# First pair's output product of layer one in seven products, pair sums and attention placed first in their queues, and no elementwise work on GpSimd

## The chip, the cores and the metric

The kernel runs on one core of a Trainium2 chip. The metric is the device time of one execution in microseconds (us). In the rows PE is TensorE, PEld its weight loads, DVE is VectorE, ACT is ScalarE, POOL is GpSimd and SP is SyncE, whose queue issues nearly all transfers.

## The reference

A linear attention feeds two feed-forward layers, all in float32, on 4608 tokens of 512 numbers.

```
q_s = softmax of q over the head's 64 numbers;  k_s = softmax of k over the sequence
kv  = k_s^T v                      (8 batches, 8 heads, 576 positions)
x   = q_s kv                       -> 4608 x 512
g   = x @ w_gate;  val = x @ w_val            (512 x 1536)
x   = (g * sigmoid(g) * val) @ w_out          (1536 x 512)      layer one
h   = max(x @ w1, x @ w2, x @ w3)             (512 x 768)
out = h @ w_out2                              (768 x 512)       layer two
```

## The kernel before

The tokens are cut into nine blocks of 512. Blocks 0, 1 and 2 are worked one at a time (stages 0 to 2). The last six are worked as three pairs (3,4), (5,6), (7,8): stages 3, 4 and 5, in the code `s`. Every operand is split into a high and a low part of a 32-bit format that TensorE takes, and each product is three matmuls (high x high, high x low, low x high).

**Seven products.** A pair multiplies in Strassen's way: a block of 2 x 2 sub-matrices in seven products in place of eight, at the price of sums on DVE and ACT. `wino_unit` does that for the products with the gate, value and W1 to W3 weights: one unit is seven products of six matmuls, 42 in all, with the operands b11, t1, t3, t2, b21, b22, t4 (made by `x_wino` from the rows `xr`), and `wino_add` (L818) and `consume` (L783, L780, L774) empty the PSUM banks and put the sums together. The output product of layer one (kind "O", weight w_out) is done in one of two ways. `outs` does eight products' worth: 12 tiles x 2 halves x 4 slices x 3 matmuls = 288 matmuls. `factors` and `out_wino` do seven: 6 pairs x 7 products x 6 matmuls = 252 matmuls, with more sums around them (`eager`, `second_job`, `fourth_job`, L757, hidden parts by L799, wide operand splits by L1726 and L1729). Which stage takes which is the tuple `OUT_WINO`.

**A pair stage has four parts.** The gate part: twelve units (gate and value) with the first output products between them. The output part: the rest of the output products. The max part: nine units (W1, W2, W3) with the first products of layer two ("P") between them. The tail: the last 96 matmuls of layer two, during which DVE, ACT and POOL make the next stage's seven operands (`x_wino`: sums L1881, high parts L452, low parts L455). Beside that, "chains" work off the attention of the next blocks in slots between the products (pkv and px on PE). Stage 3 alone also makes the transformed weights, which it stores for stages 4 and 5 (`make_job`, L681 and L685).

**What sets the order.** A planner in Python places every instruction on a time line for each engine, with fixed costs (for a 128 x 512 tile: DVE 0.69, POOL 1.55, ACT 0.62), and the instructions are then written out in order of the planned times, which is the order of each engine's queue. `do` places an instruction in the first free gap, `best` on the engine that ends first (DVE or POOL, the latter only in the pair stages), and `soon` books a gap but writes the instruction at the time at which its inputs are there, ahead of what was placed before.

Of the kernel before, what the change touches and what calls it, by code (L numbers as in the profile page):

```python
# [21 lines left out]
def linear_attention_moe_moe_kernel(  # L22
# [23 lines left out]
    nc = tc.nc  # L46
# [798 lines left out]
    EASY = ()  # L845
# [186 lines left out]
    def advance(ch):  # L1032
        off = 0.45 * (ch is chains[1]) / 1.8
        while ch["steps"] and ch["steps"][0][0] != "P" and (ch["t"] <= clock[0] + LOOK[len(marks) - 1] or ch.get("bank")):
# [23 lines left out]
            elif e == "G":  # L1058
                t, i = gap("G", ch["t"] - SWITCH, dur + 2 * SWITCH)
                busy["G"].insert(i, (t, t + dur + 2 * SWITCH))  # L1060
                t = max(t + SWITCH, ch["t"])
                at(t, fn)
                ch["t"] = t + dur + LAT
            elif e == "B":
                ch["t"] = best(ch["t"], {"D": dur, "G": 2.0 * dur}, fn)
            elif e in ("D+", "D="):
                t, ch["i"] = take(ch["t"])
                ch["t"] = do("D", t, dur, fn, ch["i"])
            else:
                ch["t"] = do(e[0], ch["t"], dur, fn)  # L1070
# [271 lines left out]
    def factor_hidden_job(use, key, home):  # L1342
# [3 lines left out]
        t = max(t, use - 9.0)  # L1346
# [8 lines left out]
        t = do("A", t, 0.62, factor_hi, key, a, home)  # L1355
        there["hid", key] = t = do("D", t, 0.69, factor_lo, key, a)
# [38 lines left out]
    def second_job(use, s, p):  # L1395
        if ("B", p, 0, 1) not in have or not (p < 2 or left("or")):
            return False
# [4 lines left out]
        if p < 2:  # L1402
            a2, then = lambda: xr_slot(6 + p), None
        else:
# [17 lines left out]
    def spare_slot(p):  # L1422
        more[p] = sb.tile([128, TB], F32, tag="or", name="t2f", bufs=4)
# [6 lines left out]

    more = {}

    def spare_slot(p):
        more[p] = sb.tile([128, TB], F32, tag="or", name="t2f", bufs=4)
# [47 lines left out]
    def hidden_job(use, key):  # L1482
        if key not in ready or not left("hh"):
            return False
        t, h = acquire("hh", max(ready[key], use - 9.0))
        if use - t < HASTE and key[1:] not in EASY:
            t = soon("A", t, 0.62, hidden_hi, key)
            there["hid", key] = t = soon("D", t, 0.69, hidden_lo, key, nc.vector)
        else:
            t = do("A", t, 0.62, hidden_hi, key)  # L1490
            there["hid", key] = t = best(t, COST, hidden_lo, key, by=use - 1.5)
# [11 lines left out]
    def consumed(t, s, kind, p, i, half, a, psum):  # L1503
# [15 lines left out]
        else:  # L1519
            t = do("D", t, 0.69, consume, kind, p, i, half, a, tmp, nc.vector)  # L1520
# [8 lines left out]
    def wino_unit(s, kind, p, late_y=False, order=range(7)):  # L1529
# [3 lines left out]
        def end(op, bank, k):  # L1533
# [7 lines left out]
            elif k == 2:  # L1541
                T[1] = bank_free[bank] = do("D", max(t, T[1]), 0.69, wino_add, kind, ("t", T["i", 1]), T["i", 1], bank, nc.vector)
            elif k == 3:
                T[0] = bank_free[bank] = do("D", max(t, T[0]), 0.69, wino_add, kind, ("t", T["i", 0]), T["i", 0], bank, nc.vector)
                o = ("s", 1, 1) if kind == "W1" else ("t", T["i", 1])
                u = best(max(T[0], T[1]), COST, wino_add, kind, o, T["i", 0], T["i", 1])
# [7 lines left out]
            else:  # L1554
                C, i = ((0, 1), None) if k == 5 else ((1, 0), T["i", 0])
                t = max(t, T[0])
                if kind != "W1" and k == 5:
# [178 lines left out]
    def out_wino(s):  # L1736
# [80 lines left out]
        HOMES = ("or", "or"), ("or", "or"), ("s00", "s01"), ("s10", "s11")  # L1817
# [9 lines left out]
        for p in range(n + 1):  # L1827
            run(p, 4, after_m4)
            if p in (1, 2):
# [13 lines left out]
        for p in range(n + 1):  # L1843
            if p == 1:
                mark(split_b22)
            if 0 < p < n:
# [104 lines left out]
    def x_wino(n):  # L1951
        op, d = XOPS[n]
        t0 = max(clock[0] - 6.0, have["x"])
        for c in range(2):
            if d is None:
                dh, half = int(op[1]) - 1, int(op[2]) - 1
                split(op, c, t0, lambda dh=dh, half=half, c=c: plain_rows(dh, half, c))
# [7 lines left out]
            differ(op, c, t, lambda c=c: plain_rows(*d[0], c), b)  # L1965
# [9 lines left out]
    OUT_WINO = (4, 5)  # L1975
# [143 lines left out]
    def plan(s):  # L2119
# [7 lines left out]
        if wide:  # L2127
            mark(lambda: at(clock[0], new_rows))
        for p in range(F1 // 2):
            if p == 2:  # L2130
                mark(lambda: begin_x(s + 1))
            for n, kind in enumerate("GV"):
                wino_unit(s, kind, p)
                if p and wide:
                    if p < F1 // 2 - 1:
                        factors(s, p - 1, 2 * n, (("acc0", "acc1"), ("acc2", "acc3"))[n])
                    if n and p < F1 // 2 - 1:
# [203 lines left out]
```

## Time and profile before

| | us |
|---|---|
| median of 3 runs (1518.18 to 1522.36) | 1520.64 |
| the profiled execution | 1522.33 |
| its span, first to last instruction | 1520.5 |
| PE busy in the span | 1458.5 (96%) |
| DVE busy | 1097.2 (72%) |
| ACT busy | 697.2 (46%) |
| POOL busy | 80.4 (5%) |

The profiled execution lies 1.7 us above the median, and 1.8 us of it lie outside the span. PE's busy time counts a matmul to its modelled end, so it hides short waits; the time of a stage is better read as the number of its matmuls times their distance, plus what is lost.

### The profile page before, as it was taken

The page shows a single profiled execution, that of the slowest core. Times are in us where ns is not written, and L with a number is a line of the kernel's source. Part 1 is how long each engine was busy: PE and PEld are TensorE (multiplying, and loading weights), DVE is VectorE, ACT ScalarE, POOL GpSimd, SP SyncE. Part 2 cuts the span into 40 slices and gives each one's busy share as a digit, 9 for nine tenths or more (in the row PEclk, how much of TensorE's full clock was granted, in tenths as well). Part 3 has the DMA queues.
Part 4 walks back from the last instruction along what each step waited for, and adds up shares of the span by engine and source line. Part 5 has one row for each costly group of instructions (what it writes and reads, how often), then busy time and mean ns, then how long its engine had stood idle before and what let it go on. Part 6 is the DMA issues. An engine that isn't in the chain of part 4 may idle for free.

```text
span 1520.5 us, 20625 instructions
## 1 busy us (share of the span) xinstructions
PE 1458.5 (96%) x6834; PEld 1177.2 (77%) x6834; DVE 1097.2 (72%) x1879; ACT 697.2 (46%) x1196; POOL 80.4 (5%) x70
## 2 busy tenths in 40 slices
PE   2899999999999999999999989999999999999998
PEld 1666688888878888878877867888877778888887
DVE  7869996787777678676579885677887755578553
ACT  3758774554566535535443344334532332245112
POOL 1000000000000000000012040000000300000000
PEclk9899999999999999999999999999999999999999
DMA  7798878878788899988578777775776576657764
GB/s 193 201 274 298 275 235 231 257 238 256 217 283 269 289 372 307 280 268 238 180 215 259 222 221 202 209 207 160 222 207 173 177 223 195 191 160 220 208 202 148
DMA packets 318729, 349.01 MB, mean 230 GB/s; under 512 B 158368, under 2 KB 197280, under 8 KB 318624
## 3 DMA queue, kind: packets, MB, share of 16 engines
q1 hardware_dynamic: 313824, 346.52, 75.2%
q10 hardware_dynamic: 4800, 1.18, 0.4%
q8 instruction: 55, 0.90, 0.3%
q14 instruction: 50, 0.41, 0.1%
HBM read 257.16 MB, written 90.44 MB: 229 GB/s over the span
## 4 chain that ended last, share of the span: by engine, by line
PE 78%; DVE 8%; DMA 6%; ACT 5%; issue 2%; SPq 1%; ACTq 0%; DVEq 0%
PE pb L715 52%; PE pacc L736 11%; PE pacc L748 4%; PE pb L736 4%; PE pb L748 3%; DMA stage<-in_moe_w_out_dram 1%; PE pkv L270 1%; PE pacc L728 1%; ACT plain L528 1%; DMA plain<-raw_V 1%; DVE hlo L803 1%; DVE tall L818 1%; DMA v_sb<-in_v_dram 1%; DMA stage<-in_moe_w_gate_dram 1%; ACT L774 1%
## 5 line engine op out<-in xcount | busy, mean ns | idle before, releaser
L715 PE MATMUL pb<-b11h,wall 128*128 128x512 f32 x756 | 270.1, 398 | 13.1 <-ACT wall L565 6.4
L818 DVE TENSOR_TENSOR tall<-tall,pb 128x512 f32<-128x512 f32 x234 | 159.9, 684 | 158.6 <-PE pb L715 146.7
L715 PE MATMUL pb<-b21h,wall 128*128 128x512 f32 x756 | 265.1, 393 | 0.0
L715 PEld LDWEIGHTS pb<-b11h,wall 128*128 128x128 f32 x756 | 142.7, 189 | 50.6 <-ACT wall L565 8.4
L715 PEld LDWEIGHTS pb<-b21h,wall 128*128 128x128 f32 x756 | 143.1, 189 | 30.7 <-ACT tall L808 0.4
L808 ACT COPY tall<-pb 128x512 f32<-128x512 f32 x117 | 68.8, 588 | 196.8 <-PE pb L715 158.6
L715 PE MATMUL pb<-b11l,wall 128*128 128x512 f32 x378 | 148.6, 393 | 0.0
L715 PE MATMUL pb<-b21l,wall 128*128 128x512 f32 x378 | 148.0, 391 | 0.0
L568 DVE TENSOR_TENSOR wall<-plain,wall 128x512 fp32r<-128x512 f32 x126 | 86.5, 689 | 38.1 <-ACT wall L565 37.5
L565 ACT CAST wall<-plain 128x512 fp32r<-128x512 f32 x126 | 77.1, 618 | 63.8 <-DVE plain L547 22.8
L736 PE MATMUL pacc<-hhi,ow 128*128 128x512 f32 x304 | 98.9, 389 | 0.1
L715 PE MATMUL pb<-t3h,wall 128*128 128x512 f32 x252 | 88.5, 392 | 3.0 <-DVE tall L818 2.9
L789 ACT CAST hhi<-tall 128x512 fp32r<-128x512 f32 x74 | 45.5, 618 | 98.3 <-DVE tall L783 79.1
L736 PE MATMUL pacc<-ow,hhi 128*128 128x512 f32 x288 | 89.0, 390 | 0.0
L715 PE MATMUL pb<-t1h,wall 128*128 128x512 f32 x252 | 88.8, 393 | 0.0
L715 PE MATMUL pb<-b22h,wall 128*128 128x512 f32 x252 | 88.7, 392 | 0.0
L715 PE MATMUL pb<-t2h,wall 128*128 128x512 f32 x252 | 88.5, 392 | 0.0
L715 PE MATMUL pb<-t4h,wall 128*128 128x512 f32 x252 | 88.0, 390 | 0.0
L715 PEld LDWEIGHTS pb<-b11l,wall 128*128 128x128 f32 x378 | 71.4, 189 | 15.2 <-issue 1.2
L715 PEld LDWEIGHTS pb<-b21l,wall 128*128 128x128 f32 x378 | 71.5, 189 | 14.5
L783 DVE TENSOR_TENSOR tall<-s,pb 128x512 f32<-128x512 f32 x81 | 54.9, 679 | 19.4 <-PE pb L715 15.1
L803 DVE TENSOR_TENSOR hlo<-tall,hhi 128x512 fp32r<-128x512 f32 x69 | 49.5, 718 | 26.4 <-ACT hhi L789 25.8
(279 smaller groups left out, 3001.5 us busy)
## 6 DMA issues: line engine op xcount, KB each, us to landing
wall<-wino_W SPq DMA_DIRECT2D x153, 256.0 KB, 3.1
wall<-wino_G SPq DMA_DIRECT2D x102, 256.0 KB, 3.2
wall<-wino_V SPq DMA_DIRECT2D x102, 256.0 KB, 3.0
ow<-parts_O SPq DMA_DIRECT2D x33, 512.0 KB, 5.5
ow<-parts_P SPq DMA_DIRECT2D x32, 512.0 KB, 5.1
wino_W<-wall SPq DMA_DIRECT2D x63, 256.0 KB, 4.5
ow<-owino SPq DMA_DIRECT2D x48, 256.0 KB, 3.5
wino_G<-wall SPq DMA_DIRECT2D x42, 256.0 KB, 4.4
```

What stands on the lines that cost most here:

```text
L270: nc.tensor.matmul(out=c["pkv"][u * D:(u + 1) * D, g, :], lhsT=lhsT, rhs=rhs, start=i == 0, stop=i == R,)
L528: nc.scalar.activation(out=plain[conv[i]], in_=high.bitcast(F32), func=AF.Abs, scale=2.0 ** -112)
L565: nc.scalar.copy(out=wall[:, i:i + 2, 0], in_=plain[kind, f].rearrange("p (a n) -> p a n", a=2))
L568: eng.tensor_tensor(out=wall[:, i:i + 2, 1], in0=plain[kind, f].rearrange("p (a n) -> p a n", a=2), in1=wall[:, i:i + 2, 0], op=ALU.subtract,)
L715: nc.tensor.matmul(out=banks[bank], lhsT=a, rhs=b, start=start and n == 0, stop=stop and n == 5, skip_group_check=True,)
L736: nc.tensor.matmul(out=banks[bank], lhsT=lhsT, rhs=rhs, start=first and n == 0, stop=last and n == 2)
L748: nc.tensor.matmul(out=banks[bank[e]], lhsT=w[:, a, es], rhs=h[b], start=first and n == 0, stop=last and n == 2, skip_group_check=True,)
L783: eng.tensor_tensor(out=hidden_tile(kind, f, half, tmp), in0=s, in1=a(), op=ALU.mult if kind == "V" else ALU.max)
L789: nc.scalar.copy(out=hid[key][0], in_=st["h", key[1], key[2], key[3]])
L803: eng.tensor_tensor(out=lo, in0=st.pop(("h", key[1], key[2], key[3])), in1=hi, op=ALU.subtract)
L808: nc.scalar.copy(out=tall[:, i], in_=banks[bank])
L818: eng.tensor_tensor(out=out_, in0=tall[:, x], in1=banks[bank] if isinstance(bank, str) else tall[:, bank], op=ALU.add)
```

## The change

It has four pieces. `OUT_WINO` becomes (3, 4, 5): the first pair does its output product in seven products too, with places of its own for two kinds of temporary tiles (in stage 3 the tiles t2f stand in s00 to s11, because the slots "or" are taken by the weights). `best` never takes POOL. `wino_add` and, from stage 3 on, `consume` are placed by `soon`; so are the steps of the attention chains in stages 3 and 4 (`HURRY`). The rest keeps the order of the shared buffers right ("hid order", "x end").

```diff
-    EASY = ()
+    HURRY = (3, 4)
...
-        if alone[0]:
-            engines = engines.replace("G", "")
+        engines = engines.replace("G", "")
         e = min(engines, key=lambda e: gap(e, t, cost[e])[0] + cost[e] + (0.4 if e == "G" else 0.0))
         return do(e, t, cost[e], fn, *a, ENG[e])
...
             elif e in ("D+", "D="):
                 t, ch["i"] = take(ch["t"])
-                ch["t"] = do("D", t, dur, fn, ch["i"])
+                ch["t"] = (soon if len(marks) - 1 in HURRY else do)("D", t, dur, fn, ch["i"])
             else:
-                ch["t"] = do(e[0], ch["t"], dur, fn)
+                ch["t"] = (soon if len(marks) - 1 in HURRY else do)(e[0], ch["t"], dur, fn)
...
+        elif tight:
+            t = max(t, have["s read"])
+            at(t - 0.01, spare_slot, p, ("s00", "s01", "s10", "s11")[p - 2])
+            a2, then = lambda: more[p], None
...
-            t = do("D", t, 0.69, consume, kind, p, i, half, a, tmp, nc.vector)
+            t = (soon if s > 2 else do)("D", t, 0.69, consume, kind, p, i, half, a, tmp, nc.vector)
+        have["s read"] = max(have.get("s read", 0.0), t)
...
-                T[1] = bank_free[bank] = do("D", max(t, T[1]), 0.69, wino_add, kind, ("t", T["i", 1]), T["i", 1], bank, nc.vector)
+                T[1] = bank_free[bank] = soon("D", max(t, T[1]), 0.69, wino_add, kind, ("t", T["i", 1]), T["i", 1], bank, nc.vector)
...
-                u = bank_free[bank] = do("D", t, 0.69, wino_add, kind, o, T["i", 0], bank, nc.vector)
+                u = bank_free[bank] = soon("D", t, 0.69, wino_add, kind, o, T["i", 0], bank, nc.vector)
...
-        HOMES = ("or", "or"), ("or", "or"), ("s00", "s01"), ("s10", "s11")
+        HOMES = (("or", "or") if s > 3 else None,) * 2 + (("s00", "s01"), ("s10", "s11"))
...
-            if p in (1, 2):
+            if s == 3 and p < 4:
+                ahead("second", 2.0, second_job, s, (5, 4, 2, 3)[p])
+            elif s > 3 and p in (1, 2):
                 ahead("second", 2.0, second_job, s, n - 2 + p)
...
-    OUT_WINO = (4, 5)
+    OUT_WINO = (3, 4, 5)
```

The tail of stage 3 on DVE, before (h_7685 and h_7996 are hidden tiles of layer two, k_sb and km belong to the attention, the operands b11 to t4 are those of stage 4):

```order
L455 TENSOR_TENSOR b11l<-xr,b11h 128x512
L803 TENSOR_TENSOR hlo<-tall,hhi 128x512
L455 TENSOR_TENSOR t1l<-tall,t1h 128x512
L1881 TENSOR_TENSOR tall<-xr 128x512
L455 TENSOR_TENSOR t1l<-tall,t1h 128x512
L803 TENSOR_TENSOR hlo<-h_7685,hhi 128x512
L455 TENSOR_TENSOR t3l<-tall,t3h 128x512 x2
```

The same place after the change (L1891 is the line that was L1881):

```order
L455 TENSOR_TENSOR b11l<-xr,b11h 128x512 x2
L803 TENSOR_TENSOR hlo<-tall,hhi 128x512
L1891 TENSOR_TENSOR tall<-xr 128x512 x2
L455 TENSOR_TENSOR t1l<-tall,t1h 128x512 x2
L803 TENSOR_TENSOR hlo<-h_7770,hhi 128x512
L1891 TENSOR_TENSOR tall<-xr 128x512 x2
L455 TENSOR_TENSOR t3l<-tall,t3h 128x512
L161 TENSOR_TENSOR tall<-k_sb 128x512
L162 TENSOR_TENSOR km<-tall 128x256
L455 TENSOR_TENSOR t3l<-tall,t3h 128x512
```

The sums L1881 that POOL did now stand in DVE's queue, between the low parts.

The start of stage 4 on ACT, before: L774 is the gate's Silu, L218 the attention's Exp, and pb_8239 is the bank that the second unit's first product waits for.

```order
L774 ACT_TABLE_LOAD
L774 ACTIVATE s<-tall 128x512
L218 ACT_TABLE_LOAD
L218 ACTIVATE k_sb<-k_sb 128x512
L774 ACT_TABLE_LOAD
L774 ACTIVATE s<-pb_8239 128x512
```

After the change (the bank is pb_8299):

```order
L218 ACTIVATE k_sb<-k_sb 128x512
L774 ACT_TABLE_LOAD
L774 ACTIVATE s<-tall 128x512
L218 ACT_TABLE_LOAD
L218 ACTIVATE k_sb<-k_sb 128x512
L218 ACTIVATE kr_sb<-kr_sb 64x256
L774 ACT_TABLE_LOAD
L774 ACTIVATE s<-pb_8299 128x512
```

One Exp moved ahead of the first Silu, and one more small Exp (kr_sb) now stands between the two Silus.

The start of stage 3's output part on DVE after the change, which before held the plain output product's few instructions (t2f and the tiles h and xr are parts of the seven products' operands, k_sb and kr_sb the attention's):

```order
L799 TENSOR_TENSOR hlo<-h_5536,hhi 128x512
L204 TENSOR_TENSOR k_sb<-k_sb,kb 128x1024
L799 TENSOR_TENSOR hlo<-h_5756,hhi 128x512
L757 TENSOR_TENSOR xr<-tall 128x512
L799 TENSOR_TENSOR hlo<-h_5982,hhi 128x512
L757 TENSOR_TENSOR t2f<-h_6613,xr 128x512
L209 TENSOR_TENSOR kr_sb<-kr_sb,kb 64x256
L799 TENSOR_TENSOR hlo<-h_6225,hhi 128x512
L757 TENSOR_TENSOR t2f<-h_6411,xr 128x512
```

Each low part (L799) is what one output product waits for, and a sum or a step of the attention stands between one and the next.

Counted over the whole program, PE has 36 matmuls of 128 x 512 fewer; POOL loses all its 35 elementwise instructions; DVE gains 71 instructions; SP gains 16 transfers, since 42 loads of 256 KB take the place of 26 (22 of 512 KB and 4 of 256 KB).

## Rows read from the trace of the kernel before

**Rows 1.** Windows, stages 1, 3, 4 and 5: length, busy time and instructions, clock, DMA.
```profile
core 0: us, PE busy (x) PEld busy (x) DVE busy (x) ACT busy (x) POOL busy (x), PEclk, DMA share, GB/s
155.00:310.00 155.00, 154.79 (x769) 124.22 (x768) 126.33 (x227) 99.81 (x172) 2.13 (x2) 1.00 0.81 242
584.26:912.84 328.58, 318.05 (x1524) 257.59 (x1522) 243.52 (x424) 145.88 (x282) 45.01 (x29) 0.99 0.78 240
912.84:1226.27 313.43, 304.67 (x1396) 248.14 (x1395) 228.89 (x356) 125.10 (x202) 19.61 (x12) 0.99 0.69 197
1226.27:1520.50 294.23, 290.46 (x1279) 239.52 (x1277) 170.16 (x250) 88.95 (x146) 0.00 (x0) 1.00 0.65 190
```

**Rows 2.** Chain that ended last: start us, us, what, stages 4 and 5.
```profile
933.18 1.32 PE pkv L270 x40
...
1397.79 38.08 PE pb L715 x168
```

**Rows 3.** Timeline of PE, one px step: start us, us, instruction.
```profile
786.39 0.28 PE L433 MATMUL px<-qthi,kvhi 128*128 128x256 f32 x1
...
787.19 0.39 PE L715 MATMUL pb<-t4h,wall 128*128 128x512 f32 x1
```

**Rows 4.** Windows, the four parts of stage 3, then of stage 4.
```profile
584.26:732.36 148.10, 146.71 (x746) 120.49 (x744) 103.27 (x195) 71.36 (x134) 9.85 (x8) 1.00 0.83 257
732.36:773.77 41.41, 40.68 (x210) 32.40 (x209) 19.83 (x35) 20.57 (x38) 1.69 (x2) 1.00 0.73 226
773.77:885.73 111.96, 107.56 (x476) 87.12 (x475) 96.04 (x168) 42.12 (x89) 18.10 (x12) 0.98 0.72 217
885.73:912.84 27.11, 23.10 (x98) 17.58 (x96) 24.38 (x27) 11.83 (x22) 15.37 (x10) 1.00 0.84 258
912.84:1045.20 132.36, 130.42 (x634) 106.93 (x632) 84.99 (x143) 51.98 (x81) 1.06 (x1) 0.99 0.73 198
1045.20:1091.54 46.34, 46.34 (x206) 38.22 (x204) 38.27 (x56) 26.87 (x43) 0.00 (x0) 1.00 0.68 213
1091.54:1199.47 107.93, 104.54 (x463) 85.44 (x462) 83.43 (x136) 33.33 (x55) 5.40 (x3) 1.00 0.64 180
1199.47:1226.27 26.80, 23.37 (x98) 17.55 (x97) 22.21 (x24) 12.92 (x25) 13.15 (x8) 1.00 0.71 237
```

**Rows 5.** Waits of PE in stages 3 and 4: us in total, times, longest.
```profile
PE pb L736 <- DVE hlo L803: 5.0, 5, 1.6
PE pb L715 <- DVE tall L818: 2.9, 3, 1.2
PE pb L715 <- DVE t2l L455: 2.3, 1, 2.3
...
PE pb L715 <- ACT s L774: 1.9, 1, 1.9
```

**Rows 6.** Window with POOL busy throughout, in the tail of stage 3.
```profile
885.10:900.00 14.90, 13.27 (x59) 10.56 (x58) 14.83 (x12) 5.40 (x10) 14.86 (x9) 1.00 0.71 215
```

**Rows 7.** Timeline of DVE inside that window.
```profile
886.90 0.68 DVE L818 TENSOR_TENSOR tall<-tall,pb 128x512 f32<-128x512 f32 x1
...
890.31 1.77 DVE L803 TENSOR_TENSOR hlo<-tall,hhi 128x512 fp32r<-128x512 f32 x1
```

**Rows 8.** Groups of DVE in stage 4's output part: busy us, mean ns, idle before.
```profile
L799 DVE TENSOR_TENSOR hlo<-h,hhi 128x512 fp32r<-128x512 f32 x14 | 9.7, 690 | 4.2 <-ACT hhi L796 4.0
...
L1729 DVE TENSOR_TENSOR b11l<-tall,b11h 128x1024 fp32r<-128x1024 f32 x1 | 1.2, 1228 | 0.3 <-ACT b11h L1726 0.3
```

**Rows 9.** Timeline of ACT at the start of stage 4.
```profile
919.93 0.63 ACT L774 ACTIVATE s<-tall 128x512 f32<-128x512 f32 x1 [2.23 <-DVE tall L818]
920.58 1.28 ACT L218 ACT_TABLE_LOAD   x1
921.87 0.63 ACT L218 ACTIVATE k_sb<-k_sb 128x512 f32<-128x512 f32 x1
922.52 1.28 ACT L774 ACT_TABLE_LOAD   x1
923.81 0.60 ACT L774 ACTIVATE s<-pb 128x512 f32<-128x512 f32 x1
```

**Rows 10.** Windows, just after PE's waits for Silu and for t2l.
```profile
925.50:928.90 3.40, 3.40 (x10) 2.63 (x9) 0.69 (x1) 2.19 (x3) 0.00 (x0) 0.50 0.28 81
782.30:785.60 3.30, 3.30 (x8) 2.62 (x9) 3.30 (x7) 0.00 (x0) 0.00 (x0) 0.50 0.40 136
```

More of the change, by code (lines that the diff above doesn't have):

```diff
@@ L1345, in factor_hidden_job @@
         t, a, then = ready[key]
-        t = max(t, use - 9.0)
+        t = max(t, use - 9.0, 0.0 if home else have.get("hid order", 0.0))
         if home == ("or", "or"):
@@ L1355, in factor_hidden_job @@
         t = do("A", t, 0.62, factor_hi, key, a, home)
+        if not home:
+            have["hid order"] = t - 0.62 - LAT + 0.01
         there["hid", key] = t = do("D", t, 0.69, factor_lo, key, a)
@@ L1395, in second_job @@
     def second_job(use, s, p):
-        if ("B", p, 0, 1) not in have or not (p < 2 or left("or")):
+        tight = s == 3
+        if ("B", p, 0, 1) not in have or not (p < 2 or tight or left("or")):
             return False
@@ L1420, in linear_attention_moe_moe_kernel, with spare_slot @@
     more = {}
-    def spare_slot(p):
-        more[p] = sb.tile([128, TB], F32, tag="or", name="t2f", bufs=4)
+    def spare_slot(p, tag="or"):
+        more[p] = sb.tile([128, TB], F32, tag=tag, name="t2f", bufs=4 if tag == "or" else 1)
     def fourth_job(use, p):
@@ L1484, in hidden_job @@
             return False
-        t, h = acquire("hh", max(ready[key], use - 9.0))
-        if use - t < HASTE and key[1:] not in EASY:
+        t, h = acquire("hh", max(ready[key], use - 9.0, have.get("hid order", 0.0)))
+        if use - t < HASTE:
+            have["hid order"] = t + 0.01
             t = soon("A", t, 0.62, hidden_hi, key)
@@ L1490, in hidden_job @@
             t = do("A", t, 0.62, hidden_hi, key)
+            have["hid order"] = t - 0.62 - LAT + 0.01
             there["hid", key] = t = best(t, COST, hidden_lo, key, by=use - 1.5)
@@ L1541, in end @@
             elif k == 2:
[L1542 removed]
+                T[1] = bank_free[bank] = soon("D", max(t, T[1]), 0.69, wino_add, kind, ("t", T["i", 1]), T["i", 1], bank, nc.vector)
             elif k == 3:
[L1544 removed]
+                T[0] = bank_free[bank] = soon("D", max(t, T[0]), 0.69, wino_add, kind, ("t", T["i", 0]), T["i", 0], bank, nc.vector)
                 o = ("s", 1, 1) if kind == "W1" else ("t", T["i", 1])
[L1546 removed]
+                u = T["c22"] = best(max(T[0], T[1]), COST, wino_add, kind, o, T["i", 0], T["i", 1])
                 if kind == "W1":
@@ L1556, in end @@
                 t = max(t, T[0])
+                if k == 6:
+                    t = max(t, T["c22"], T["c12"])
                 if kind != "W1" and k == 5:
@@ L1845, in out_wino @@
                 mark(split_b22)
-            if 0 < p < n:
+            if 0 < p < n and HOMES[p - 1]:
                 ahead("hid2", 2.0, factor_hidden_job, (s, "O", p + 1, 6), HOMES[p - 1])
@@ L1956, in x_wino @@
                 dh, half = int(op[1]) - 1, int(op[2]) - 1
-                split(op, c, t0, lambda dh=dh, half=half, c=c: plain_rows(dh, half, c))
+                have["x end"] = max(
+                    have.get("x end", 0.0), split(op, c, t0, lambda dh=dh, half=half, c=c: plain_rows(dh, half, c))
+                )
                 continue
@@ L1964, in x_wino @@
                 b = lambda c=c: plain_rows(*d[1], c)
-            differ(op, c, t, lambda c=c: plain_rows(*d[0], c), b)
+            have["x end"] = max(have.get("x end", 0.0), *differ(op, c, t, lambda c=c: plain_rows(*d[0], c), b))
     def x_plain(j, dh):
@@ L2127, in plan @@
         if wide:
-            mark(lambda: at(clock[0], new_rows))
+            mark(lambda: at(max(clock[0], have["x end"]), new_rows))
         for p in range(F1 // 2):
```

7 lines of the change are left out of this document (3 added, 4 removed).

## The prediction

> **What bounds the kernel now.** I read the busy shares first: PE 96%, DVE 72%. PE bounds the kernel, so the time is its matmuls plus what PE loses. Stages 0 to 2 keep their PE order, and the additions to DVE, ACT and SP begin with stage 3, so I look at stages 3 and 4 [rows 1]. Stage 5 has no POOL work and takes 294.2 us with its 1278 matmuls (289.7) and the last stores, so it loses almost nothing; I leave it as it is [rows 1].
>
> What a stage loses comes from counting. In an undisturbed run 168 matmuls take 38.08 us, 0.2267 us each [rows 2]. A pkv step of the attention costs 1.32 us [rows 2], a px step 0.80 (786.39 to 787.19) [rows 3], or 0.68 where it is one piece of three matmuls. Stage 3 has 21 units of 42, 288 output and 144 layer-two matmuls: 1314, or 297.8 us; four pkv and eight px steps add 11.7. Its length is 328.6 us [rows 1], so **19.0 us are lost**. Stage 4 has 36 matmuls fewer (289.7 us), two pkv and eight px steps (8.5), and 313.4 us: **15.2 us lost**. By parts, in the same way [rows 4]: stage 3's gate part 2.7 (624 matmuls, three pkv), output part 2.0 (168, one pkv), max part 9.0 (426, eight px), tail 5.35 (96); stage 4's 4.6 (552, two pkv), 0.1 (204), 5.5 (426, eight px) and 5.0 (96).
>
> Which waits these are is in the list of PE's waits [rows 5]: 5.0 us for low parts of hidden tiles (L803, all in the tails), 2.9 for PSUM sums (L818), 2.3 once for t2l, 1.9 once for Silu. Then the clock: right after the t2l wait and right after the Silu wait the granted clock is 0.50, that is 1.2 GHz, for 3.3 and 3.4 us [rows 10]. Half of that, some 1.7 us each, is lost behind either wait.
>
> Why DVE is late in the tails: while POOL works without pause from 885.1 to 900, DVE is busy 14.83 of 14.90 us with only 12 instructions [rows 6]. A subtraction of two SBUF tiles takes 1.77 us there; a sum that takes one operand from PSUM takes its usual 0.68 [rows 7]. Undisturbed, the former takes 0.69 [rows 8]. So 12 instructions worth 8.3 us cost 14.8: POOL's 14.9 us cost DVE 6.5, and its nine tiles in that window would have cost DVE 6.2 itself. POOL's help there is worth nothing.
>
> **The change part by part.**
>
> *Seven products in stage 3.* 288 matmuls become 252: 36 x 0.2267 = **8.2 us less on PE**. Transfers: 42 loads of 256 KB take the place of 24 tiles' 512 KB, 10.8 for 12.6 MB. That stage's DMA share is 0.78 now, and the shares of stages 3 to 4 are under stage 1's 0.81, where PE was fed [rows 1]; I cost the 16 more issues on SP's queue at nothing. If that cover goes, one late load of an output weight would cost what any wait in the list does, 1 to 2 us.
>
> *What DVE takes on.* The order shows 71 instructions more, POOL's 35 among them. They are 57 of 128 x 512 at 0.69, 15 of 128 x 1024 at 1.22 [rows 8], less two short copies: 57 us. Of these 8 belong to stage 4 (POOL's 11 there), so 49 to stage 3. Against that the stretching goes. POOL's 45.0 us in stage 3 [rows 1] at the rate found (6.5 per 14.9) are at most 20 us; five all-reduces are in it, so I take 18. DVE in stage 3: 243.5 + 49 - 18 = 274.5 us. In a stage of about 309 us that is 89%.
>
> Does PE wait at 89%? The nearest rows: stage 1 has 81.5% with PE busy 154.79 of 155 us, and stage 4's output part 83% with 0.1 us lost [rows 1, 4]. On the other side is the window in which DVE was full: PE was busy 13.27 of 14.90, 11% idle [rows 6]. The heaviest place is stage 3's output part, where one low part per product (1.36 us of PE) stands beside sums, four steps of the attention and the first weights of W1. Stage 4 does its own there in 38.3 us of 46.3 [rows 4]; some 7 us come on top, so about 45 in 47.5. Bounds for this part: 0.1, and 11% of 47.5 = 5.2; I take 2.0, since the low parts run up to three tiles ahead of PE.
>
> *Sums and attention first.* `soon` moves no work. It takes the PSUM sums (2.9 us of waits) and the attention out from behind other work; what stands behind them are low parts, weights' low parts (L685) and hidden parts, which have more slack. Together with POOL gone, stage 3's max part loses its t2l wait with its half clock (4.0 of 9.0: those operands now come out of the output part as in stage 4, where nothing is lost at that seam) and most of the rest. Bounds 0.1 (the clean part of stage 4) and the present 9.0 and 5.5; I take 2.0 and 1.7.
>
> *The tails.* From b11l on DVE has in stage 3 now 28 tile instructions and 2 us of attention, 21 us at 0.69, and starts at about 888, between the two instructions of [rows 7]. It ends near 909; t4, the last operand, is needed when six products of the next stage are done, 885.7 + 21.8 + 6 x 1.36 = 915.7. The low parts of the hidden tiles stand between the sums; the last three come some 10 us in, when their products are due from about 14 us in. Bounds 0.1 and the present 5.35 and 5.0; I take 0.8 and 0.7.
>
> *The gate parts.* At the start of stage 4 the second unit's first product waits for Silu out of its bank. The row order there is Silu, table load, Exp, table load, Silu [rows 9]: that ends 11.6 us after the stage's start, when its first unit takes 9.5. After the change the second (small) Exp stands in that row as well: 0.4 more by size (bounds 0 and a full Exp's 0.63). So this wait stays, 2.4 for 2.1, and the half clock behind it too: 4.6 becomes 5.0. In stage 3's gate part DVE is fuller, but its sums go first: 2.7 becomes 3.0.
>
> On ACT's tables the Trainium skill (ScalarE: Activation LUTs, What ACT_TABLE_LOAD costs) says that a switch takes 1.28 us for the load and 1.38 more for a drain. Here the load takes 1.28 and the next instruction starts 0.01 us later [rows 9], so the drain does not show; by the page the three loads would end about 2.8 us later and the time would be 1498.
>
> *Sum.* Stage 3 keeps 3.0 + 2.0 + 2.0 + 0.8 = 7.8 of 19.0; stage 4 keeps 5.0 + 0.1 + 1.7 + 0.7 = 7.5 of 15.2. Gain: 8.2 + 11.2 + 7.7 = 27.1 us. The profiled execution took 1522.3 (1.8 of it outside its span, 1.7 above the median): 1522.3 - 27.1 = **1495 us**.
>
> **The rivals.**
>
> *DVE becomes what PE waits for in stage 3, and new waits there are as long as the old.* For it: 89% is above every long stretch in which PE was fed. Against it: the planner's 0.69 and 0.62 agree with the undisturbed rows, and what it did not know, POOL's cost to DVE, is gone. Then only 8.2 + 7.7 remain: 1506 (1502 to 1514).
>
> The Trainium skill (Perfetto Trace Analysis, Optimizing Scalar/DVE Operations) speaks for this rival: with DVE saturated, moving work to ScalarE or even GpSimd may make sense; it adds that the two share a read port, so that it might not help. The trace bears out the second half (1.77 for 0.69); with the first half the time is that rival's 1506.
>
> *DVE can't keep up at all, and the kernel is slower.* If in-order waits (DVE standing before an Exp that waits for its table, 1.28 us [rows 9], with bank sums behind it) hold DVE to a usable share u, stage 3 takes 274.5/u. It eats up stage 4's gain when it takes 336.3, that is at u = 82%, about what stages 1 and 4 show as possible at least. At u = 78% stage 3 takes 352 and the kernel 1538.
>
> *Nearly all losses go*, only the Silu wait and its clock stay: stage 3 keeps 2.8, stage 4 5.3, gain 34 us, 1488 or less.
>
> *The order changes and the waits don't:* the tails' waits come from ACT, not DVE. Of PE's tail waits 5.0 us end with DVE's L803 [rows 5], so I give it little; the kernel would still save the 8.2: 1514, the slow end of the first rival.
>
> **How the numbers follow.** Forecast (1488 to 1502) 0.60; DVE-limited stage 3 (1502 to 1514) 0.22; nearly all losses go (under 1488) 0.08; no change (within 0.3%, 4.6 us, about what a measurement of this kernel can tell from none) 0.05; slower 0.05. Faster is 0.60 + 0.22 + 0.08 = 0.90. The range 1485 to 1510 leaves out about 0.05 below and 0.13 above.
>
> **What would show it.** Right: POOL's row holds only memsets and all-reduces; no subtraction on DVE above 0.75 us; in stage 3 36 matmuls fewer, L803 gone from the tails' waits, stage 3 at 308 to 311 us and stage 4 at 305 to 307; one wait of 2.3 to 2.5 us for Silu at stage 4's start with the clock at 0.50 behind it. Wrong: waits of PE for L799 or L685 in stage 3's output and max parts, a second stretch at 0.50 behind one of them, DVE over 95% there. A gap for DMA before an output product would say that the smaller loads come late.

## The result and the profile after

The changed kernel takes 1501.42 us (median of 4 runs, 1500.72 to 1502.07) against 1520.63 of the kernel before (1518.18 to 1522.36): a ratio of 0.9875, 95% interval 0.9858 to 0.9892, so 19.2 us faster. Its profiled execution took 1501.56, of which the span is 1499.5. The forecast was 1495.0 with a range of 1485 to 1510; the time lies in the range and 6.4 us above the forecast, and 19.2 us were gained where the sum had 27.1.

The page's busy row and its row of PE's granted clock in 40 slices (9 is 90% or more), of the changed kernel:

```profile
PE 1443.3 (96%) x6798; PEld 1169.4 (78%) x6798; DVE 1110.1 (74%) x1950; ACT 702.0 (47%) x1204; POOL 23.9 (2%) x35
...
PEclk9899999999999999999999999999999999999999
```

PE has 36 matmuls fewer (6834 before), and POOL holds memsets and all-reduces alone, 35 instructions. Next, windows of the changed kernel: stages 3, 4 and 5, then the four parts (gate, output, max, tail) of stage 3 and of stage 4; the columns are those of [rows 1]. In stage 3 the gate part now has 552 matmuls where it had 624, and the output part 204 for 168, so these two are compared by what they lose and not by their length.

```profile
582.84:893.01 310.17, 305.54 (x1487) 250.23 (x1486) 260.84 (x479) 152.43 (x291) 6.06 (x4) 1.00 0.80 244
893.01:1204.26 311.25, 304.17 (x1396) 250.01 (x1394) 225.49 (x370) 123.20 (x202) 2.12 (x2) 0.99 0.69 202
1204.26:1499.50 295.24, 290.67 (x1279) 239.45 (x1277) 168.20 (x250) 88.92 (x146) 0.00 (x0) 1.00 0.63 191
...
582.84:713.96 131.12, 130.39 (x673) 106.96 (x672) 106.89 (x207) 66.79 (x128) 4.10 (x3) 1.00 0.87 262
713.96:761.97 48.01, 48.01 (x245) 39.25 (x244) 42.58 (x71) 31.62 (x55) 1.96 (x1) 1.00 0.73 213
761.97:871.21 109.24, 105.34 (x476) 86.08 (x474) 92.79 (x173) 41.75 (x85) 0.00 (x0) 1.00 0.74 231
871.21:893.01 21.80, 21.80 (x97) 17.94 (x96) 18.57 (x31) 12.27 (x23) 0.00 (x0) 1.00 0.84 267
893.01:1029.81 136.80, 131.95 (x634) 108.06 (x633) 87.07 (x147) 49.46 (x80) 2.12 (x2) 0.98 0.72 200
1029.81:1076.05 46.24, 46.24 (x206) 38.29 (x205) 38.23 (x56) 26.78 (x43) 0.00 (x0) 1.00 0.69 215
1076.05:1182.50 106.45, 104.22 (x464) 85.64 (x462) 81.24 (x139) 33.64 (x55) 0.00 (x0) 1.00 0.64 182
1182.50:1204.26 21.76, 21.76 (x98) 18.02 (x96) 18.94 (x31) 13.33 (x24) 0.00 (x0) 1.00 0.79 282
```

Stage 3 took 328.58 us [rows 1] and takes 310.17, inside the 308 to 311 of the forecast. Stage 4 took 313.43 and takes 311.25, where 305 to 307 was forecast. Both tails are clean now: 96 matmuls of 0.2267 us are 21.76, and they take 21.80 and 21.76 (27.11 and 26.80 in [rows 4]). Stage 4's gate part is the one that became longer: 132.36 in [rows 4], 136.80 now.

The waits of PE from stage 3 on, us in total, times, longest:

```profile
PE pb L715 <- ACT tall L827: 2.6, 1, 2.6
PE pb L715 <- DVE b21l L1737: 2.5, 3, 1.0
PE pb L715 <- ACT s L774: 2.2, 1, 2.2
PE pb L715 <- DVE tall L818: 2.2, 3, 1.5
PE px L433 <- DVE tall L818: 1.7, 2, 0.9
```

Against [rows 5] the 5.0 us of low parts (L803) and the 2.3 for t2l are gone. The Silu wait (L774) is there, as forecast. Two entries of over 2 us are new. One is ACT's row copy L827. The other is b21l, once in each of stages 3, 4 and 5.

The first, on ACT's timeline at the start of stage 4 (start us, us, instruction; in brackets the wait ahead of it and what ended it):

```profile
891.87 1.07 ACT L827 COPY tall<-pb 128x512 f32<-128x512 f32 x2 [1.12 <-DMA out_dram<-tall]
...
897.88 0.58 ACT L827 COPY tall<-pb 128x512 f32<-128x512 f32 x1 [3.90 <-DMA out_dram<-tall]
...
904.61 0.63 ACT L774 ACTIVATE s<-tall 128x512 f32<-128x512 f32 x1 [3.06 <-DVE tall L818]
905.26 1.28 ACT L218 ACT_TABLE_LOAD   x1
906.56 0.63 ACT L218 ACTIVATE k_sb<-k_sb 128x512 f32<-128x512 f32 x1
907.10 0.40 ACT L218 ACTIVATE kr_sb<-kr_sb 64x256 f32<-64x256 f32 x1
907.51 1.28 ACT L774 ACT_TABLE_LOAD   x1
908.80 0.60 ACT L774 ACTIVATE s<-pb 128x512 f32<-128x512 f32 x1
```

The copy that empties a bank of stage 3's last products stands 3.90 us, until a store of an earlier copy has left the slot in which it wants to write. The first product of t3 needs that bank. PE meets this wait and the Silu wait as follows (timeline of PE):

```profile
895.51 0.39 PE L715 MATMUL pb<-t1h,wall 128*128 128x512 f32 x1
898.52 0.50 PE L715 MATMUL pb<-t3h,wall 128*128 128x512 f32 x1 [2.63 <-ACT tall L827]
...
906.85 0.39 PE L715 MATMUL pb<-t4h,wall 128*128 128x512 f32 x1
909.46 0.79 PE L715 MATMUL pb<-b11h,wall 128*128 128x512 f32 x1 [2.22 <-ACT s L774]
```

Counted from where the next matmul would have started, 0.23 us after the last, PE loses 2.78 and 2.38 us.

Windows behind these two waits, and for contrast behind one of 1.46 us (L818) in stage 4's max part; the column after POOL is the granted clock:

```profile
899.10:902.40 3.30, 3.30 (x9) 2.59 (x8) 1.01 (x2) 2.40 (x3) 0.00 (x0) 0.50 0.43 130
909.60:912.90 3.30, 3.30 (x8) 2.60 (x9) 0.41 (x1) 0.84 (x2) 0.00 (x0) 0.52 0.01 4
1110.80:1114.10 3.30, 3.30 (x15) 2.73 (x16) 3.19 (x9) 0.59 (x1) 0.00 (x0) 1.00 0.97 294
```

Behind either long wait the clock is at 1.2 GHz for nearly all of the 3.3 us, and 8 or 9 matmuls stand where 15 stand at 2.4 GHz. The length of a wait does not tell this by itself: in the kernel with eight products below, PE loses 2.54 us by the same count to a load at 665, in stage 3's gate part, and from 667.5 to 670.8 its clock is 1.00.

### The profile page after: what moved, and what is told of

Its sections match the earlier page's. It is cut to its first block, busy times and chain, and to the rows that moved or that the text cites. A ratio compares the mean times of both kernels' runs of the same rounds, so it can differ in the third digit from the quotient of the medians.

```text
span 1499.5 us, 20638 instructions
## 1 busy us (share of the span) xinstructions
PE 1443.3 (96%) x6798; PEld 1169.4 (78%) x6798; DVE 1110.1 (74%) x1950; ACT 702.0 (47%) x1204; POOL 23.9 (2%) x35
## 4 chain that ended last, share of the span: by engine, by line
PE 78%; DVE 5%; ACT 3%; DMA 3%; issue 1%; SPq 1%; ACTq 0%; DVEq 0%
PE pb L715 52%; PE pacc L736 10%; PE pacc L748 6%; PE pb L748 5%; PE pb L736 3%; PE pkv L270 1%; DVE tall L818 1%; DMA plain<-raw_V 1%; ACT L218 1%; PE px L434 1%; PE px L435 1%; PE px L433 1%; ACT L774 0%; DMA twos<-sums_W 0%; DMA qown<-in_q_dram 0%
## 5 line engine op out<-in xcount | busy, mean ns | idle before, releaser
L818 DVE TENSOR_TENSOR tall<-tall,pb 128x512 f32<-128x512 f32 x234 | 159.8, 684 | 165.3 <-PE pb L715 151.1
L715 PEld LDWEIGHTS pb<-b21h,wall 128*128 128x128 f32 x756 | 141.9, 188 | 29.7
L748 PE MATMUL pacc<-hhi,ow 128*128 128x512 f32 x248 | 82.0, 389 | 0.0
L783 DVE TENSOR_TENSOR tall<-s,pb 128x512 f32<-128x512 f32 x81 | 55.0, 680 | 18.0 <-PE pb L715 14.4
L748 PE MATMUL pb<-hhi,ow 128*128 128x512 f32 x216 | 68.3, 390 | 0.0
L789 ACT CAST hhi<-tall 128x512 fp32r<-128x512 f32 x62 | 38.4, 620 | 63.4 <-DVE tall L783 48.3
```

The lines of the kernel that those rows point to most:

```text
L715: nc.tensor.matmul(out=banks[bank], lhsT=a, rhs=b, start=start and n == 0, stop=stop and n == 5, skip_group_check=True,)
L748: nc.tensor.matmul(out=banks[bank[e]], lhsT=w[:, a, es], rhs=h[b], start=first and n == 0, stop=last and n == 2, skip_group_check=True,)
L783: eng.tensor_tensor(out=hidden_tile(kind, f, half, tmp), in0=s, in1=a(), op=ALU.mult if kind == "V" else ALU.max)
L789: nc.scalar.copy(out=hid[key][0], in_=st["h", key[1], key[2], key[3]])
L818: eng.tensor_tensor(out=out_, in0=tall[:, x], in1=banks[bank] if isinstance(bank, str) else tall[:, bank], op=ALU.add)
```

## The experiments

Each set of runs had the kernel before in it, with medians of 1519.3 to 1520.6 us. So where two kernels come from different sets, as the changed kernel and those below do, up to some 1.4 us of a difference can be due to that. Times of stages are those of one profiled execution.

**GpSimd back.** Everything else as in the changed kernel; `best` may take POOL in the pair stages again.

```diff
-        engines = engines.replace("G", "")
+        if alone[0]:
+            engines = engines.replace("G", "")
```

> The changed kernel with one piece undone: in the pair stages the planner may choose GpSimd again (it then gives it 54 tile operations, more than the 35 of before, since DVE has more to do). Theory of the prediction: GpSimd's work stretches DVE's two-SBUF-input operations from 0.69 to 1.77 us, so the tails of stages 3 and 4 lose 4 to 6 us each again and the max parts some more: 1511 to 1520. Rival, DVE-limited stage 3: relief for DVE, which is at 89% there, outweighs it: 1495 to 1501.

Measured: 1531.07 us, ratio to the kernel before 1.0073 (1.0057 to 1.0088). That is 29.7 us more than the changed kernel, beyond either expectation. POOL has 63 elementwise instructions, where 54 were expected. The busy line of its page, and two of DVE's groups in stages 3 and 4:

```profile
PE 1454.8 (95%) x6798; PEld 1171.6 (77%) x6798; DVE 1127.5 (74%) x1892; ACT 696.0 (45%) x1197; POOL 129.7 (8%) x98
...
L818 DVE TENSOR_TENSOR tall<-tall,pb 128x512 f32<-128x512 f32 x156 | 106.4, 684 | 90.5 <-PE pb L715 81.2 <-ACT wall L681 5.6 <-ACT tall L808 1.9
L803 DVE TENSOR_TENSOR hlo<-tall,hhi 128x512 fp32r<-128x512 f32 x8 | 9.9, 1234 | 4.2 <-ACT hhi L789 4.2
```

DVE has 58 instructions fewer than in the changed kernel (1950) and is busy 17.4 us longer (1110.1). The low parts L803 of the tiles tall, with two SBUF operands, take 1234 ns where the changed kernel has 680 (8.2 us for 12 in the same stages); other groups with two such operands are lengthened less (L783 into h 965 for 692, L803 of the tiles h 773 for 687). The sums with one operand in PSUM take 684, as without POOL (683). What PE waits for most are DVE's instructions (L818 13.4 us in four entries, hlo of L803 3.9, qtlo 3.3), and no entry is POOL's.

**No "first".** All `soon` that the change brought are `do` again.

```diff
-            t = (soon if s > 2 else do)("D", t, 0.69, consume, kind, p, i, half, a, tmp, nc.vector)
+            t = do("D", t, 0.69, consume, kind, p, i, half, a, tmp, nc.vector)
...
-                u = bank_free[bank] = soon("D", t, 0.69, wino_add, kind, o, T["i", 0], bank, nc.vector)
+                u = bank_free[bank] = do("D", t, 0.69, wino_add, kind, o, T["i", 0], bank, nc.vector)
```

> The changed kernel with one piece undone: bank-emptying sums and attention are placed by do, as before, in place of soon. Theory of the prediction: the order is worth a few us, mostly in the max parts (waits for L818): 1503 to 1508. Rival, the order carries most of the gain: 1511 or more. Second rival, the order hurts: sums written ahead of an operand's low part make PE wait 0.8 to 1.0 us for b21l in each of the three stages, so that without it the kernel is at 1497 to 1500.

Measured: 1500.75 us, ratio 0.9881 (0.9866 to 0.9896): no different from the changed kernel, and outside all three expectations. But the stages differ: by the starts of their first products, stage 3 takes 318.2 us (310.2 with "first") and stage 4 302.6 (311.3). The profiled execution took 1504.9, 4.2 above the median; ahead of stage 3 it was 5.8 us longer than the changed kernel's. No wait for b21l is left, as the second rival said, but in stage 3 longer ones for L818 and L783 stand in the max part. In this pair of kernels the order is worth 8 us in stage 3, and stage 4 is 8.6 longer with it; the next experiment shows that this 8.6 does not belong to the order as such.

**Eight products.** `OUT_WINO = (4, 5)`.

> The changed kernel with one piece undone: stage 3 does its output product in eight products' worth of matmuls again. Theory of the prediction: 36 matmuls come back, 8.2 us, and DVE is freer, which gives back little: 1508 to 1512. Rival, DVE-limited stage 3: the 29 us of sums taken off DVE give back as much as the matmuls cost: 1499 to 1503.

Measured: 1509.81 us, ratio 0.9933 (0.9917 to 0.9950). In all, the seven products are worth 8.4 us; the forecast had 8.2. By stages it is another sum. The windows of stages 3 and 4 of this kernel:

```profile
584.32:911.06 326.74, 317.38 (x1524) 257.80 (x1522) 234.64 (x442) 148.43 (x286) 4.90 (x4) 0.99 0.76 239
911.06:1213.82 302.76, 300.52 (x1395) 247.82 (x1394) 224.80 (x370) 122.73 (x201) 2.13 (x2) 1.00 0.70 205
```

With seven products stage 3 is 16.6 us shorter, twice what the 36 matmuls are, and stage 4 is 8.5 longer. Here stage 4 has the sums first too and neither the wait for L827 nor the one for Silu at its start: its gate part takes 128.2 us for 136.8.

**The kernel before without GpSimd.** The unconditional replacement of the first experiment, put into the kernel before.

> The kernel before with one piece alone: the planner never chooses GpSimd. Theory of the prediction: the tails' losses of 5.35 and 5.0 us go, and the max parts lose some 2 to 5 us less: 1506 to 1511. Rival: DVE's longer queue makes new waits of the same size: 1517 to 1522.

Measured: 1513.95 us, ratio 0.9959 (0.9944 to 0.9974), 5.3 us less than the kernel before beside it (1519.26) and between the two expectations. The tails shrink from 27.1 and 26.8 to 23.5 and 21.8 us, but the Silu wait at stage 4's start grows to 3.9 us, and stage 3's max part gains nothing (113.4 us). Against the kernel with eight products above, which differs in the order "first" and the plumbing that goes with the change, stage 3 takes 325.6 us here for 326.7 and stage 4 308.4 for 302.8: with eight products stage 3 gains nothing by the order, and it is stage 4 that is shorter with it.

**The slot of the row copies.** Who makes the new wait? The planner gives a slot back 2.5 us after the copy, when the store is to be issued; here it counts on 5 us more.

```diff
-            drop(i, sync(t + 2.5, store_rows, j, m, i))
+            drop(i, sync(t + 2.5, store_rows, j, m, i) + 5.0)
```

> Kernel after, with one number changed: the planner counts the slot of a stored row copy as free 5 us later, so the next copy into the same slot is planned later. My theory (the 2.78 us that PE loses at 895.74 in stage 4's gate part come from a row copy, L827 on ACT, that stands 3.90 us before a store still reading its slot, with the next casts behind it): this wait and the half clock behind it go, 2.8 + 1.7 = 4.5 us less, stage 4 at about 306.8 us and the kernel at 1497. Rival (that cast is late since DVE's or ACT's row is full there, and the store only ends last): another wait of 2 to 3 us takes its place before the same products, stage 4 stays at 310 to 312 and the kernel at 1500 to 1503.

Measured: 1498.03 us, ratio 0.9856 (0.9843 to 0.9869). Stage 4's window:

```profile
894.34:1201.13 306.79, 302.31 (x1395) 248.94 (x1394) 224.80 (x369) 122.49 (x200) 2.13 (x2) 0.99 0.69 204
```

Stage 4 is 4.5 us shorter, as expected of the wait and its half clock, and no wait took its place there. The kernel gained 3.4; the rest went in one late load in stage 3's tail and in the start (0.7 later).

**The seam to the max part.** DVE's timeline of the changed kernel ahead of b21l in stage 3:

```profile
764.81 1.23 DVE L1737 TENSOR_TENSOR t2l<-xr,t2h 128x1024 fp32r<-128x1024 f32 x1 [0.18 <-ACT t2h L1734]
765.96 0.68 DVE L1714 TENSOR_TENSOR xr<-pacc,xr 128x512 f32<-128x512 f32 x1
766.56 0.68 DVE L818 TENSOR_TENSOR tall<-tall,pb 128x512 f32<-128x512 f32 x1
767.15 1.22 DVE L757 TENSOR_TENSOR xr<-xr 128x1024 f32<-128x1024 f32 x1
768.29 0.68 DVE L818 TENSOR_TENSOR tall<-tall,pb 128x512 f32<-128x512 f32 x1
768.88 1.22 DVE L1737 TENSOR_TENSOR b21l<-xr,b21h 128x1024 fp32r<-128x1024 f32 x1
```

Two bank sums stand ahead of b21l, which PE waits for at 769.02. The first max unit alone gets plain order:

```diff
+        put = soon if tuple(order) == tuple(range(7)) else do
...
-                u = bank_free[bank] = soon("D", t, 0.69, wino_add, kind, o, T["i", 0], bank, nc.vector)
+                u = bank_free[bank] = put("D", t, 0.69, wino_add, kind, o, T["i", 0], bank, nc.vector)
```

> Kernel after, but in the first max unit of each stage the bank sums are put in plain planned order, no longer first, so that b21l stands ahead of them on DVE. My theory (the waits for b21l of 1.13, 0.93 and 0.93 us at the start of the max parts of stages 3, 4 and 5 come from sums that were put ahead of it): all three go, about 3.0 us less, the kernel at 1498.5. Rival (the sums that now come later hold up their banks, or b21l is late anyway): the waits stay or change their name to L818, the kernel at 1500 to 1503.

Measured: 1501.90 us, ratio 0.9882 (0.9864 to 0.9900): nothing. The three waits for b21l are gone, and stage 5 is 1.4 us shorter (290.1 to the end of its last product), but stage 3 takes 318.0 for 310.2. Its waits from the max part to the next stage's first units:

```profile
PE px L433 <- DVE tall L818: 4.5, 4, 2.0
PE pb L715 <- DVE tall L818: 2.2, 1, 2.2
PE pb L736 <- DVE hlo L803: 2.0, 2, 1.7
```

The sums that came later hold the next products: the rival was right in stage 3, my theory in stage 5. Stage 4 takes 305.4 us for 311.3, though its own max part is 1.3 longer: the waits for L827 and for Silu at its start are both gone, and the edit says nothing of them. They come and go with what stands before them.

**Keys later.** The last pair's keys start 24 us later, so that their Exps leave the place between the first Silus.

```diff
-        chains[2]["t"] = clock[0]
+        chains[2]["t"] = clock[0] + 24.0 * (s == 5)
```

> Kernel after, but the chain of the keys in the last pair starts 24 us later, so that no Exp with its two table loads stands between the first two Silus of stage 4. My theory (the Silu wait is those two loads of 1.28 us and the Exp): the wait of 2.38 us at 907.08 and the half clock behind it go, some 4 us less, the kernel at 1497 to 1498. Rival (the Exps, moved, make another Silu or sum late, or the attention comes late for its px steps): a wait of 2 to 4 us shows up later in stage 4, the kernel at 1500 to 1504.

Measured: 1494.17 us, ratio 0.9831 (0.9817 to 0.9844), 7.3 us less than the changed kernel, more than expected. ACT's timeline at the start of stage 4, and the stage's window:

```profile
899.44 1.28 ACT L774 ACT_TABLE_LOAD   x1
901.50 0.63 ACT L774 ACTIVATE s<-tall 128x512 f32<-128x512 f32 x1 [0.78 <-DVE tall L818]
902.04 0.58 ACT L774 ACTIVATE s<-pb 128x512 f32<-128x512 f32 x1
...
893.60:1196.45 302.85, 300.62 (x1396) 247.73 (x1394) 225.40 (x372) 120.80 (x198) 2.13 (x2) 1.00 0.71 206
```

One table load stands where three stood, and the second Silu follows the first by 0.54 us instead of 4.19. PE does not wait for L827 any more either, although nothing was done to the stores; how the slots changed hands there was not followed up. Both waits with both half clocks are 2.78 + 2.38 + 2 x 1.7 = 8.6 us, and stage 4 is 8.4 shorter, with the sums and the attention still first in it.

**The three together.**

> The three edits before this one together: slot kept 5 us longer, bank sums of the first max unit in plain order, keys of the last pair 24 us later. If the three waits have separate causes the gains add up: 4.5 + 3.0 + 4.0 = 11.5 us, the kernel at about 1490, which is what the forecast's rival of nearly all losses gone would have been. Rival (the waits share DVE's and ACT's full rows at the start of stage 4, so that taking one away lengthens another): half of that or less, 1495 to 1501.

Measured: 1496.23 us, ratio 0.9844 (0.9827 to 0.9860), 5.2 us less than the changed kernel and 2.1 more than with the late keys alone, in the rival's range. Stage 4 takes 301.7 us and stage 5 289.8 to the end of its last product, both as the theory wants, but stage 3 has 314.3: the seam's plain order costs there again, and not at the start of stage 4, where the rival looked for it.

**The three, with plain order at the seam in stages 4 and 5 alone.**

```diff
+        put = soon if s == 3 or tuple(order) == tuple(range(7)) else do
```

> Kernel after with the keys of the last pair 24 us later, the slot of row copies kept 5 us longer, and plain order for the bank sums of the first max unit in stages 4 and 5 alone (stage 3 keeps them first). My theory (each stage is decided by its own order: stage 3 wants the sums first, stages 4 and 5 don't): stage 3 at about 310, stage 4 at 302, stage 5 at 290, against 310.2, 302.9 and 291.8 with the late keys alone: 2 to 3 us less than that kernel, 1491 to 1492. Rival (what plain order gains there was made by the other order in stage 3): stages 4 and 5 as with the late keys alone, 1494 to 1495.

Measured: 1490.76 us, ratio 0.9813 (0.9800 to 0.9826). This is 10.7 us below the changed kernel and 29.0 below the kernel before beside it (1519.73), just under the 1491 to 1492 of the theory. Its windows of stages 3, 4 and 5, then of stage 4's gate part:

```profile
583.14:892.96 309.82, 305.37 (x1487) 250.50 (x1486) 261.69 (x479) 153.55 (x292) 6.07 (x4) 1.00 0.80 246
892.96:1194.62 301.66, 300.66 (x1396) 247.74 (x1394) 226.06 (x372) 121.31 (x198) 2.13 (x2) 1.00 0.71 208
1194.62:1488.10 293.48, 289.84 (x1279) 239.76 (x1277) 168.55 (x250) 88.93 (x146) 0.00 (x0) 1.00 0.64 191
...
892.96:1021.16 128.20, 128.20 (x633) 105.97 (x632) 87.62 (x149) 47.53 (x76) 2.13 (x2) 1.00 0.76 212
```

Stage 4's gate part has PE busy without a pause. Most of the gain was there with the late keys alone (1494.17); stage 4 is 1.2 and stage 5 2.0 us shorter than in that kernel. The time is close to the 1488 of the prediction's rival in which nearly all losses go.

**Seven products alone; first alone.** Why does GpSimd cost 5.3 us in the kernel before and 29.7 in the changed one? These two complete the eight combinations: the first undoes both other parts, the second is GpSimd back together with eight products.

> The kernel before with the seven products alone: GpSimd may take work in pairs, sums and attention in plain order. Theory A (GpSimd's harm grows with DVE's load: the seven products bring some 50 us of elementwise work into stage 3, and GpSimd then stretches DVE where it is full): slower than before or no gain, stage 3 some 325 us or more, the kernel at 1520 to 1530. Theory B (GpSimd's harm in the kernel with its work put back comes from putting sums first, which shifts what GpSimd has taken): the seven products give their 8 us here too, 1510 to 1514.

Measured: 1508.67 us, ratio 0.9929 (0.9917 to 0.9941).

> The kernel before with sums and attention first alone: eight products in the first pair's output, GpSimd may take work in pairs. Theory A (GpSimd's harm grows with DVE's load): about as before, 1517 to 1522, since the order by itself is worth nothing. Theory B (putting sums first makes GpSimd's harm larger): 1528 to 1538.

Measured: 1539.20 us, ratio 1.0130 (1.0116 to 1.0145). Theory B is the one that fits in both, though each time lies a little outside its range (1510 to 1514, 1528 to 1538). The medians in us, from three sets of runs:

| | eight products, plain order | eight, first | seven, plain | seven, first |
|---|---|---|---|---|
| GpSimd allowed | 1519.7 (before) | 1539.2 | 1508.7 | 1531.1 |
| GpSimd barred | 1514.0 | 1509.8 | 1500.8 | 1501.4 (changed) |

Read down a column, barring GpSimd is worth 5.7, 29.4, 7.9 and 29.7 us. Read along a row, "first" costs 19.5 and 22.4 with GpSimd, and without it gives 4.2 and -0.6. The seven products give 8.1 to 13.2 everywhere. With seven products and no GpSimd the whole gain is there; the order adds nothing to it. The page's busy line of the kernel with first alone:

```profile
PE 1462.3 (95%) x6834; PEld 1178.6 (77%) x6834; DVE 1094.2 (71%) x1851; ACT 688.9 (45%) x1189; POOL 128.1 (8%) x99
```

POOL takes 99 instructions and 128.1 us where the kernel before has 70 and 80.4: `best` sent POOL more. In the planner, `soon` hands on an earlier time while the place in DVE's row stays booked, so POOL should end first more often; that is read from the code and was not tried.

**Sums kept on DVE.** Among POOL's new instructions there are 21 sums (L783, L818). If they do the harm, barring these alone should take it away.

```diff
-            t = best(t, COST, consume, kind, p, i, half, a, tmp)
+            t = best(t, COST, consume, kind, p, i, half, a, tmp, engines="D")
-                u = T["c22"] = best(max(T[0], T[1]), COST, wino_add, kind, o, T["i", 0], T["i", 1])
+                u = T["c22"] = best(max(T[0], T[1]), COST, wino_add, kind, o, T["i", 0], T["i", 1], engines="D")
```

> The kernel with sums and attention first alone (eight products, GpSimd allowed), but the sums of two SBUF tiles (L818) and the hidden parts (L783) may only go to DVE, as they all did in the kernel before; low parts, x_wino's sums and the attention may still go to GpSimd. Theory (putting work first made the planner send GpSimd these 21 instructions, 1.6 to 1.8 us each, which stand in the chain that empties the banks, and they are what cost it 19.5 us): back to 1515 to 1525. Rival (any tile work on GpSimd does that harm beside a DVE whose order is by the time of its inputs): still 1532 to 1540.

Measured: 1533.44 us, ratio 1.0093 (1.0076 to 1.0110). Only 5.8 of the 19.5 us come back; the rival held and my theory is wrong in the main. POOL still has 80 instructions, 99.8 us; one group of DVE that shows it, in stages 3 and 4:

```profile
L418 DVE TENSOR_TENSOR qtlo<-tall,qthi 128x512 fp32r<-128x512 f32 x8 | 8.7, 1081 | 0.7 <-ACT qthi L414 0.7
```

In the kernel before this group takes 678 ns. The attention's multiplications on POOL (L237, L256) number 13 here and 12 with first alone, where the kernel before has 6; with first alone the group takes 1127 ns.

## Why the prediction was near, and where it was off

*Stage 3* came as forecast: 310.2 us for 309.1. It loses 8.8 us for 7.8, by the prediction's counting. Inside it the terms were less good, and that they cancel is luck. The output part at DVE's fullest loses 0.4 (2.0 forecast), the gate part 2.0 (3.0), the tail 0.04 (0.8). The max part loses 6.3 (2.0): the t2l wait with its half clock went, as forecast, but waits of 0.2 to 1.0 us for b21l, for L818 ahead of px and of products, and for qt stayed or came. DVE was busy 260.84 us in stage 3, 84%, and not 274.5: the rival of a DVE that becomes the bound was further off than the estimate said. One reason stands in DVE's timeline above: back to back, an instruction of 0.68 us starts 0.59 or 0.60 after the one ahead of it (765.96, 766.56, 767.15), so 0.69 for each, added up, is too much.

*The seven products* gave 8.4 us for 8.2, and PE's list of waits has none for a load from stage 3 on. The agreement is luck: 8.4 is 16.6 less in stage 3 and 8.5 more in stage 4 (the rest lies in stages 0 to 2 and in the difference between executions and medians). The prediction's 8.2 is the matmuls alone; in stage 3 the eight products also bring longer waits, 11.2 us lost in the max part for 6.3 and three waits for loads of output weights, 3.3 in all, and how these divide was not tried. (The prediction's 10.8 MB is 11.0 in the unit of its 12.6; nothing hangs on it.)

*The tails* were read rightly. The kernel before without GpSimd shows that POOL's absence alone takes 3.6 and 5.0 us out of them.

*Sums and attention first* was a wrong reason. The prediction put most of the max parts' gain down to it. Without GpSimd the order gives 4.2 us with eight products, and with seven nothing: stage 3 is 8 us shorter with it and stage 4 8.6 longer. Of those 8.6, 7.2 lie in stage 4's gate part, where the two long waits are, and 1.4 in its max part. The two waits are not the price of the order as such: with the order kept, stage 4 takes 302.8 us with eight products and 302.9 with the late keys. Its statement that what stands behind the sums has more slack fails at the seams, where b21l stands behind two sums and is the next product's operand.

*The step that was mis-sized* is stage 4: 7.7 us of gain forecast, 2.2 measured. Of its terms the gate part is off most, 9.0 lost for 5.0, and then the max part, 4.0 for 1.7. The Silu wait was forecast with its table loads (2.4, measured 2.38, half clock behind it). What was not seen is a second wait of 2.78 us with a second half clock just ahead of it: the row copy L827 for a slot still being stored. The longer slot shows that cause, since only this wait went with it in stage 4. Why the changed kernel meets it and neither the kernel with eight products, nor the one without "first", nor the one with plain order at the seam does so was not tried; they put other work in those slots, and that is an argument and no more.

*The rest:* stage 5 lost 1.0 us more (b21l, and the order), which the prediction left as it was; stages 0 to 2 were 1.4 us shorter in this execution, and no experiment here is about them. Together: 27.1 - 1.0 - 5.5 - 1.0 + 1.4 = 21.0, the difference of the two spans. The medians differ by 19.2. The prediction took its 27.1 from a profiled execution 1.7 us above the median; taken from the median they would have given 1493.5, so 1.7 us of the nearness is luck too.

*GpSimd.* That POOL's help is worth nothing was right and said too little: it costs. With "first" it costs 29.4 and 29.7 us. The prediction had cited the Trainium skill (Perfetto Trace Analysis, Optimizing Scalar/DVE Operations), which allows for GpSimd where DVE is full and warns of the shared port. The trace agrees with the warning (1234 ns beside 680 for L803), and in all four pairs the kernel with GpSimd is the slower one. How the harm divides between DVE's stretched instructions and results that come late from POOL itself stays open: the last experiment shows only that the 21 sums are 5.8 us of it. The traces make the stretching the larger suspect. Against the median of the same kind of instruction in the changed kernel, DVE's instructions of stages 3 and 4 take some 32 us too long in the kernel before, 54 with GpSimd back, 49 with first alone and 44 with the sums kept on DVE. DVE's own waits that end with POOL are at most 2.3 us there, and none of PE's does; ACT's are 8 to 21 in the last three.

*The table loads.* The prediction weighed a drain behind each switch, by the Trainium skill (ScalarE: Activation LUTs, What ACT_TABLE_LOAD costs). The trace after again shows none: the Silu ahead ends at 905.24, the load of 905.26 at 906.54, and the Exp starts at 906.56.

## What to carry to other kernels

Cost a reordering for each stage, by what stands behind the work that goes first, and try it beside each of the other pieces: here the same rule made stage 3 8 us shorter and stage 4 8.6 longer with seven products, but with eight stage 3 1.2 longer and stage 4 5.6 shorter, largely because waits at the start of stage 4 came and went with what stood ahead of them. Taking away those waits was worth more (7.3 us) than choosing the order by stages. When a change takes out the waits of one place, look at the next seam for a resource that gave no wait until then, such as a buffer that its planner calls free while a store still reads it. A helper engine is to be judged with the planner that feeds it: a change of order that seemed free gave it 59% more busy time (128.1 us for 80.4), and made that help cost five times as much.

## What the runs showed of the hardware

Where GpSimd works on SBUF tiles, DVE's instructions are lengthened by kind: of those with two SBUF operands the groups hit most go from 680 to 1234 ns (L803) and from 678 to 1081 (L418) in the mean, while the sums with one operand in PSUM (L818) stay at 683 to 684. A store of 256 KB from a row copy's slot landed 5.1 us after its issue in the median around the start of stage 4 (2.5 to 6.4, 8 stores), while the plan counts the slot as free from the issue on. And taking away a wait that is followed by the half clock gave more than its own length: 2.78 us of wait in the slot experiment brought stage 4 4.5 us. Not every wait of such a length is followed by it: behind one of 2.54 us for a load the clock stayed 1.00 (eight products, 667.5 to 670.8).
